# The gate of a feed-forward layer, merged in another order from the third chunk on

## The chip, the cores and the metric

The kernel runs on one core of a Trainium2 chip. Its engines work side by side, each through its own instructions in order: PE (TensorE, matmuls; PEld is its weight loads), DVE (VectorE), ACT (ScalarE), POOL (GpSimd) and SP, which issues the DMAs. PSUM is the memory that PE writes its products to; here it has eight banks of 128 x 512 floats. The metric is the time of one execution on the device in microseconds (us). Before the change it is 1264.36 us, the median of three runs (1263.34 to 1266.16).

## The reference

Attention over 8 batches of 8 heads, each with 512 local tokens and 32 global ones: a global token attends to all tokens, a local one to the global ones and to local ones at most 32 positions away. Its result `x` (4608 tokens of width 512) goes through a gated feed-forward layer of width 1536, which is what the change is in:

```python
gate = 1.0 / (1.0 + np.exp(-(x @ w_gate)))
val = x @ w_val
return (gate * val @ w_out).astype(np.float32)
```

## The kernel before

The tokens are worked in chunks. The first batch is two chunks of 256 tokens, each further batch one of 512, and the 256 global tokens are a last chunk. The feed-forward of a chunk is twelve items, one for each 128 columns of the hidden layer; the items of the first two chunks are interleaved, so items 0 to 23 are theirs, and from item 24 on each chunk's twelve follow one another. Matrices are split into a high and a low part in a reduced float format, and each product is three matmuls (high by high, low by high, high by low).

One item is: twelve matmuls into a PSUM tile `bank_g` (the gate's sum z), twelve into `bank_v` (the value), both at L380; then the gate and the product with the value; then a split of the result into `hh`; and, one item later, twelve matmuls of `hh` with `w_out` into four banks that collect the output (`bank_o`, L414). The stream yields after every four matmuls, and there the attention of a later chunk is slipped in: scores (L237, L317, L319), the row's maximum (L251, L322 to L324), exponentials (L254, L326, L327), scaling (L225), transposition on PE (L268, L335), the split of the transposed weights (L279 on ACT, then L280 on DVE), and the product with the values (L298, L299, L348), which leaves through L301 and L302. During the last two chunks there is no attention left to do.

The sigmoid is computed as half of (1 + |tanh(z/2)|) times exp(min(z, 0)); the half is taken with the output. For items from 24 on: ACT takes the tanh (L388) into `th`, DVE the minimum (L393) into `mn`, ACT the exponential of `mn` (L394) and the size of `th` (L395). L396 on DVE then makes (1 + `th`) x `mn`, and when `bank_v` is complete, L398 multiplies by it. L400 (ACT) and L401 (POOL) split the result.

`th` and `mn` have one buffer each, `hh` two. The PSUM tiles `bank_x`, `bank_y`, `bank_g` and `bank_v` share four banks: a new tile gets a bank when the last reader of the old one is done, and PE waits for that reader. The order of each engine's instructions is set when the program is built, by a scheduler that places each instruction by its dependences and an estimate of times, so a changed dependence can also move other instructions. SP, which issues the DMAs, and PE keep their order here; DVE, ACT and POOL do not.

Of the kernel before, what the change touches and what calls it, by code (L numbers as in the profile page):

```python
# [12 lines left out]
ALU = mybir.AluOpType  # L13
# [38 lines left out]
NF = DF // P  # L52
# [4 lines left out]
def kernel(ctx, tc, qk, v, w_gate, w_val, w_out, out_l, out_g):  # L57
    nc = tc.nc
# [306 lines left out]
    def ffn_stream(items):  # L365


        prev = None
        wo = None
        for n_it in range(len(items) + 1):  # L370
            if n_it < len(items):
                C, f = items[n_it]
                ntok, x0, xt = C["ntok"], C["x0"], C["xt"]()
                fs = slice(f * P, (f + 1) * P)
                for w, nm in ((wg, "bank_g"), (wv, "bank_v")):
                    acc = ps.tile([P, 512], F32, name=nm, tag="att", bufs=4)[:, 0:ntok]
                    n = 0
                    for a, c in ((0, 0), (1, 0), (0, 1)):
                        for t in range(KT):
                            nc.tensor.matmul(acc, w[a][:, t, fs], xt[:, c, t, x0:x0 + ntok],  # L380
                                             start=n == 0, stop=n == 11)
                            n += 1
                        if n < 12:
                            yield ntok / 512
                    if nm == "bank_g":
                        th = ffn.tile([P, 512], F32, name="th", bufs=1)[:, 0:ntok]
                        mn = ffn.tile([P, 512], F32, name="mn", bufs=1)[:, 0:ntok]
                        nc.scalar.activation(th, acc, AF.Tanh, scale=0.5)  # L388
                        if n_it < 2 * NF and n_it % 2:
                            nc.scalar.activation(mn, acc, AF.Relu, scale=-1.0)  # L390
                            nc.scalar.activation(mn, mn, AF.Exp, scale=-1.0)
                        else:
                            nc.vector.tensor_scalar(mn, acc, 0.0, None, op0=ALU.min)  # L393
                            nc.scalar.activation(mn, mn, AF.Exp)  # L394
                        nc.scalar.activation(th, th, AF.Abs)  # L395
                        nc.vector.scalar_tensor_tensor(th, th, 1.0, mn, op0=ALU.add, op1=ALU.mult)  # L396
                    else:
                        nc.vector.tensor_tensor(th, acc, th, op=ALU.mult)  # L398
                        hh = ffn.tile([P, 2, 512], F32R, name="hh", bufs=2)
                        nc.scalar.copy(hh[:, 0, 0:ntok], th)  # L400
                        nc.gpsimd.tensor_tensor(hh[:, 1, 0:ntok], th, hh[:, 0, 0:ntok].bitcast(F32), op=ALU.subtract)  # L401
                    yield ntok / 512
                if not (wo is not None and items[n_it - 1][1] == f):
                    wo = ffn.tile([P, 2, DM], F32R, name="wo", bufs=2)
                    nc.sync.dma_start(wo.bitcast(F32), wo_dram[f])
            if prev is not None:
                C2, f2, ph, pwo = prev
                nt = C2["ntok"] // P
                if f2 == 0:
                    C2["o"] = [ps.tile([P, DM], F32, name=f"bank_o{C2['o0'] + t}") for t in range(nt)]  # L410
                o_ps = C2["o"]
                for i, (a, c) in enumerate(((0, 0), (1, 0), (0, 1))):
                    for t in range(nt):
                        nc.tensor.matmul(o_ps[t], ph[:, a, t * P:(t + 1) * P], pwo[:, c],  # L414
                                         start=f2 == 0 and i == 0, stop=f2 == NF - 1 and i == 2)
                    if f2 == NF - 1 and i == 2:
                        for t in range(nt):
                            ob = ffn.tile([P, DM], F32, name="ob", bufs=2)
                            if t % 2:
                                nc.scalar.mul(ob, o_ps[t], 0.5)  # L420
                            else:
                                nc.vector.tensor_scalar(ob, o_ps[t], 0.5, None, op0=ALU.mult)
                            nc.sync.dma_start(C2["dst"][t * P:(t + 1) * P, :], ob)
                    yield nt / 4
            prev = (C, f, hh, wo) if n_it < len(items) else None
# [97 lines left out]
    for dt in ffn_stream(items):  # L523
        now += dt
        while queue and queue[0][0] <= now:
            queue.pop(0)[2]()
# [55 lines left out]
```

## Time and profile before

| | us |
|---|---|
| median of three runs | 1264.36 |
| the profiled execution, time | 1262.67 |
| its span, first to last instruction | 1260.8 |
| PE busy | 1223.5 (97%) |
| PE weight loads busy | 998.6 (79%) |
| DVE busy | 878.9 (70%) |
| ACT busy | 782.9 (62%) |
| POOL busy | 571.1 (45%) |

The mean granted clock of PE was 0.989; after the first 200 us it is 1.00. In the profile's rows, `out<-in` names the tiles, x is the count, and what stands behind an arrow is what ended the idle time before the instruction. Matmuls are pipelined, so the time of a group of them reaches a little past the start of the next. L numbers are lines of the kernel before the change.

### The profile page before, as it was taken

What the parts mean: (1) busy time and instruction counts of PE and PEld (TensorE: products, weight loads), DVE (VectorE), ACT (ScalarE), POOL (GpSimd) and SP (SyncE); (2) the same over time, 40 slices, a digit from 0 to 9 for tenths busy, and PEclk for the clock granted to TensorE, in tenths of its full rate; (3) what the DMA queues carried; (4) which work ended last, traced back from release to release, by engine and by line L of the source; (5) the groups of instructions that cost most, each with busy time, mean ns of one, the idle gap of its engine ahead of it and who ended that gap; (6) DMA issues with size and microseconds to landing.
All of it is one profiled execution on the core that took longest, in us unless ns stands there. A gap on an engine that the chain in (4) does not pass through costs nothing.

```text
span 1260.8 us, 20601 instructions
## 1 busy us (share of the span) xinstructions
PE 1223.5 (97%) x6884; PEld 998.6 (79%) x6884; DVE 878.9 (70%) x2433; ACT 782.9 (62%) x1899; POOL 571.1 (45%) x573
## 2 busy tenths in 40 slices
PE   8899989999999999999999999999999999999998
PEld 6677768788778877888788877888788877888897
DVE  6888977757876778758776778767875787632232
ACT  5686766756666666656765766656665666532333
POOL 2444545535555455545554455535554545311111
PEclk9798999999999999999999999999999999999999
DMA  6686754333333333333334333333333332122243
GB/s 232 215 264 219 255 172 125 107 97 108 92 103 113 113 92 108 109 106 112 100 86 120 121 100 100 108 112 109 91 107 114 108 92 88 51 84 67 67 134 117
DMA packets 59497, 151.90 MB, mean 120 GB/s; under 512 B 6144, under 2 KB 19456, under 8 KB 59392
## 3 DMA queue, kind: packets, MB, share of 16 engines
q1 hardware_dynamic: 59392, 150.59, 39.3%
q8 instruction: 54, 0.88, 0.3%
q14 instruction: 51, 0.42, 0.1%
HBM read 135.36 MB, written 15.20 MB: 119 GB/s over the span
## 4 chain that ended last, share of the span: by engine, by line
PE 73%; DVE 16%; ACT 6%; issue 4%; DMA 1%; POOL 0%; POOLq 0%; DVEq 0%; ACTq 0%; SPq 0%
PE bank_g L380 19%; PE bank_v L380 18%; PE bank_o L414 18%; PE bank_x L237 4%; PE bank_y L268 4%; DVE p_buf L225 3%; DVE th L396 2%; PE bank_y L335 2%; PE bank_x L348 2%; DVE pg_buf L225 2%; PE bank_x L298 2%; ACT s_sb L254 1%; PE bank_x L299 1%; PE bank_x L317 1%; DVE pt L280 1%
## 5 line engine op out<-in xcount | busy, mean ns | idle before, releaser
L380 PE MATMUL bank_g<-xt,wg 128*128 128x512 f32 (+1 forms) x1440 | 340.2, 371 | 1.8 <-DVE th L398 1.8
L380 PE MATMUL bank_v<-xt,wv 128*128 128x512 f32 (+1 forms) x1440 | 332.7, 368 | 3.0 <-DVE pt L280 2.7
L414 PE MATMUL bank_o<-wo,hh 128*128 128x512 f32 x1224 | 334.1, 404 | 0.8 <-ACT hh L400 0.4
L380 PEld LDWEIGHTS bank_g<-xt,wg 128*128 128x128 f32 x1440 | 238.6, 191 | 41.7 <-issue 3.5
L380 PEld LDWEIGHTS bank_v<-xt,wv 128*128 128x128 f32 x1440 | 237.8, 190 | 40.7 <-PE bank_y L319 3.1
L414 PEld LDWEIGHTS bank_o<-wo,hh 128*128 128x128 f32 x1224 | 214.1, 189 | 38.9 <-ACT hh L400 1.2
L401 POOL TENSOR_TENSOR hh<-th,hh 128x512 fp32r<-128x512 f32 (+1 forms) x120 | 137.6, 1147 | 200.7 <-ACT hh L400 199.8
L254 ACT ACTIVATE s_sb<-s_sb,nm 128x224 f32<-128x224 f32 x240 | 113.8, 475 | 142.9 <-DVE nm L251 141.8
L225 DVE TENSOR_SCALAR p_buf<-s_sb,r 128x128 f32<-128x128 f32 (+1 forms) x443 | 151.8, 386 | 4.2 <-PE bank_y L268 0.4
L393 DVE TENSOR_SCALAR mn<-bank_g 128x512 f32<-128x512 f32 (+1 forms) x108 | 67.3, 623 | 110.8 <-ACT th L388 109.4
L396 DVE SCALAR_TENSOR_TENSOR th<-th,mn 128x512 f32<-128x512 f32 (+1 forms) x120 | 102.0, 850 | 59.9 <-ACT mn L394 53.6
L206 POOL TENSOR_TENSOR kl<-qk_raw,qk_hi 128x704 fp32r<-128x704 f32 x52 | 88.4, 1700 | 116.0 <-ACT qk_hi L205 116.0
L303 POOL TENSOR_TENSOR x<-t 64x256 f32<-64x256 f32 x104 | 76.1, 732 | 142.7 <-DVE t L302 138.5
L388 ACT ACTIVATE th<-bank_g 128x512 f32<-128x512 f32 (+1 forms) x120 | 63.5, 530 | 98.0 <-PE bank_g L380 96.5
L400 ACT CAST hh<-th 128x512 fp32r<-128x512 f32 (+1 forms) x120 | 66.5, 554 | 68.6 <-DVE th L398 68.1
L251 DVE CUSTOM_DVE_ANT_0 s_sb<-bank_x,masks 128x224 f32<-128x224 f32 x240 | 83.8, 381 | 12.6 <-PE bank_x L237 8.2
L208 POOL TENSOR_TENSOR qk_hi<-qk_raw,qk_hi 64x256 fp32r<-64x256 f32 x104 | 87.8, 863 | 4.1
L268 PE MATMUL bank_y<-ident,p_buf 128*128 128x128 f32 x496 | 78.7, 279 | 9.4 <-DVE p_buf L225 5.1
L268 PEld LDWEIGHTS bank_y<-ident,p_buf 128*128 128x128 f32 x496 | 60.3, 142 | 29.5 <-ACT pg_buf L326 6.6
L257 DVE TENSOR_SCALAR r<-sm 128x2 f32<-128x2 f32 x128 | 29.3, 229 | 75.8 <-ACT s_sb L254 74.1
L205 ACT CAST qk_hi<-qk_raw 128x1248 fp32r<-128x1248 f32 x52 | 64.1, 1233 | 22.3 <-PE bank_y L319 22.2
L398 DVE TENSOR_TENSOR th<-bank_v,th 128x512 f32<-128x512 f32 (+1 forms) x120 | 72.4, 603 | 5.0 <-PE bank_v L380 1.3
(111 smaller groups left out, 1994.6 us busy)
## 6 DMA issues: line engine op xcount, KB each, us to landing
wo<-wo_dram SPq DMA_DIRECT2D x116, 512.0 KB, 3.5
qk_raw<-in_qk_dram SPq DMA_DIRECT2D x104, 312.0 KB, 4.5
v_raw<-in_v_dram SPq DMA_DIRECT2D x52, 256.0 KB, 2.6
out_dram<-ob SPq DMA_DIRECT2D x34, 256.0 KB, 2.9
xt<-in_w_gate_dram SPq DMA_DIRECT2D x12, 512.0 KB, 4.7
xt<-in_w_val_dram SPq DMA_DIRECT2D x12, 512.0 KB, 4.1
xt<-in_w_out_dram SPq DMA_DIRECT2D x12, 512.0 KB, 4.9
v_nat<-in_v_dram SPq DMA_DIRECT2D x8, 512.0 KB, 4.5
```

The costliest lines, as they stand in the source:

```text
L206: nc.gpsimd.tensor_tensor(kl, t[:, K0:Q1], hi[:, K0:Q1].bitcast(F32), op=ALU.subtract)
L208: nc.gpsimd.tensor_tensor(hi[64:128, r], t[64:128, r], hi[64:128, r].bitcast(F32), op=ALU.subtract)
L225: nc.vector.tensor_scalar(out, in_, by, None, op0=ALU.mult)
L251: anchor[0] = nc.vector.tensor_tensor_reduce(out=s_sb[:, i], in0=s_ps[:, i, 0:WIN], in1=masks[:, m], scale=-0.125, scalar=3.0e38, op0=ALU. ...
L254: nc.scalar.activation(s_sb[:, i], s_sb[:, i], AF.Exp, bias=nm[:, i:i + 1], scale=-1.0, accum_out=sm[:, i:i + 1])
L268: nc.tensor.transpose(pt_ps[:, 2 * i + t], pb[:, i, t * P:(t + 1) * P], ident)
L303: nc.gpsimd.tensor_tensor(dst, t0[:, :, 0], t0[:, :, 1], op=ALU.add)
L380: nc.tensor.matmul(acc, w[a][:, t, fs], xt[:, c, t, x0:x0 + ntok], start=n == 0, stop=n == 11)
L396: nc.vector.scalar_tensor_tensor(th, th, 1.0, mn, op0=ALU.add, op1=ALU.mult)
L398: nc.vector.tensor_tensor(th, acc, th, op=ALU.mult)
L401: nc.gpsimd.tensor_tensor(hh[:, 1, 0:ntok], th, hh[:, 0, 0:ntok].bitcast(F32), op=ALU.subtract)
L414: nc.tensor.matmul(o_ps[t], ph[:, a, t * P:(t + 1) * P], pwo[:, c], start=f2 == 0 and i == 0, stop=f2 == NF - 1 and i == 2)
```

## The change

For items from 24 on, the value's product is first multiplied by the exponential, in place in PSUM, and only then by one plus the tangent's size. The first two chunks keep the old order.

```diff
                         nc.scalar.activation(th, th, AF.Abs)
-                        nc.vector.scalar_tensor_tensor(th, th, 1.0, mn, op0=ALU.add, op1=ALU.mult)
+                        if n_it < 2 * NF:
+                            nc.vector.scalar_tensor_tensor(th, th, 1.0, mn, op0=ALU.add, op1=ALU.mult)
                     else:
-                        nc.vector.tensor_tensor(th, acc, th, op=ALU.mult)
+                        if n_it < 2 * NF:
+                            nc.vector.tensor_tensor(th, acc, th, op=ALU.mult)
+                        else:
+
+                            nc.vector.tensor_tensor(acc, acc, mn, op=ALU.mult)
+                            nc.vector.scalar_tensor_tensor(th, th, 1.0, acc, op0=ALU.add, op1=ALU.mult)
                         hh = ffn.tile([P, 2, 512], F32R, name="hh", bufs=2)
```

The two new lines are L403 and L404 of the changed kernel. Both read `bank_v`, so its bank comes free only after the second. The first place shown is on DVE, about the middle of the run, where a head's scaled weights (`p_buf`, L225) are done and the split of the transposed ones (`pt`, L280) follows; `mg` belongs to the softmax of the global tokens. Before:

```order
L225 TENSOR_SCALAR p_buf<-s_sb,r 128x96
L396 SCALAR_TENSOR_TENSOR th<-th,mn 128x512
L280 TENSOR_TENSOR pt<-bank_y,pt 128x512
L398 TENSOR_TENSOR th<-bank_v,th 128x512
L322 TENSOR_REDUCE mg<-bank_x 32x1
L323 TENSOR_REDUCE mg<-bank_y 32x1
L324 TENSOR_SCALAR mg<-mg 32x1
L329 TENSOR_SCALAR mg<-sg 32x1
```

The same place on DVE after the change:

```order
L225 TENSOR_SCALAR p_buf<-s_sb,r 128x96
L280 TENSOR_TENSOR pt<-bank_y,pt 128x512
L403 TENSOR_TENSOR bank_v<-bank_v,mn 128x512
L322 TENSOR_REDUCE mg<-bank_x 32x1
L404 SCALAR_TENSOR_TENSOR th<-th,bank_v 128x512
L323 TENSOR_REDUCE mg<-bank_y 32x1
L324 TENSOR_SCALAR mg<-mg 32x1
L302 TENSOR_TENSOR t_7206<-bank_x,t_7206 64x512
L329 TENSOR_SCALAR mg<-sg 32x1
```

The product of `th` and `mn` no longer stands ahead of L280; the last product now stands behind a reduction, L322, and L302 has moved up. The second place is on DVE too, a little earlier in the run, where the softmax weights of the global tokens (`pg_buf`, L225) are scaled. Before:

```order
L396 SCALAR_TENSOR_TENSOR th<-th,mn 128x512
L329 TENSOR_SCALAR mg<-sg 32x1
L398 TENSOR_TENSOR th<-bank_v,th 128x512
L302 TENSOR_TENSOR t_7014<-bank_x,t_7014 64x512
L280 TENSOR_TENSOR pt<-bank_y,pt 128x512
L330 RECIPROCAL mg<-mg 32x1
L225 TENSOR_SCALAR pg_buf<-pg_buf,mg 32x576
L251 ISA s_sb,nm<-bank_x,masks 128x224
```

And after:

```order
L329 TENSOR_SCALAR mg<-sg 32x1
L403 TENSOR_TENSOR bank_v<-bank_v,mn 128x512
L302 TENSOR_TENSOR t_7013<-bank_x,t_7013 64x512
L280 TENSOR_TENSOR pt<-bank_y,pt 128x512
L404 SCALAR_TENSOR_TENSOR th<-th,bank_v 128x512
L330 RECIPROCAL mg<-mg 32x1
L251 ISA s_sb,nm<-bank_x,masks 128x224
L251 ISA nm 128x1
L225 TENSOR_SCALAR pg_buf<-pg_buf,mg 32x576
```

Here the product of `th` and `mn` no longer stands ahead of L302 and L280; the last product and one L251 (a row's maximum, two rows) now stand between L280 and `pg_buf`. On ACT, at the first place, the copy that L302 needs (L301) now stands ahead of the split of `hh`. On POOL, at the same place, the second half of that split (L401 before, L407 after) now stands behind the two L208.

## The prediction

> **What bounds the kernel now.** I read the page's head and its chain of work first, then the busy time in two stretches, then who waits for whom inside them.
>
> ```profile
> PE 73%; DVE 16%; ACT 6%; issue 4%; DMA 1%; POOL 0%; POOLq 0%; DVEq 0%; ACTq 0%; SPq 0%
> ```
>
> TensorE (PE) carries 73% of the chain that ends last, VectorE (DVE) 16%. The profiled execution took 1262.67 us, of which its span is 1260.8 and 1.9 lies around it (the table above). The median of the runs shown, 1264.36, lies 1.69 higher, so I work out a difference on the trace and take it off the median.
>
> The change touches the items from the third chunk on. The first of their gates is on DVE at 271 us; up to 1110 us the attention of a later chunk runs beside them, after that the feed-forward is alone. Busy time by stretch (length, then PE, PEld, DVE, ACT, POOL):
>
> ```profile
> 270.00:1110.00 840.00, 830.95 (x4530) 676.49 (x4529) 628.57 (x1767) 552.51 (x1287) 425.54 (x429) 1.00 0.35 101
> 1110.00:1255.00 145.00, 144.81 (x762) 122.88 (x760) 40.13 (x72) 48.47 (x95) 22.91 (x23) 1.00 0.31 98
> ```
>
> PE idles 9.05 us in the first stretch and 0.19 in the second. The work itself is untouched, so at best the change returns PE's waits. Who PE waited for between 270 and 1110 us (total, times, longest):
>
> ```profile
> PE bank_x L298 <- DVE pt L280: 4.4, 11, 0.6
> PE bank_v L380 <- DVE pt L280: 2.7, 6, 0.5
> PE bank_y L335 <- DVE pg_buf L225: 1.2, 6, 0.2
> ```
>
> All three are DVE, and DVE works in order: what matters is what stands ahead of L280 and L225. The two instructions that the change replaces, in the same stretch (min/median/max ns; then by form with busy us, mean, idle before):
>
> ```profile
> L396 DVE SCALAR_TENSOR_TENSOR th<-th,mn x73: 691/693/1705, 271.1 to 1106.1; 128x512 f32<-128x512 f32 x73
> L398 DVE TENSOR_TENSOR th<-bank_v,th x73: 672/680/694, 272.3 to 1106.9; 128x512 f32<-128x512 f32 x73
> L396 DVE SCALAR_TENSOR_TENSOR th<-th,mn 128x512 f32<-128x512 f32 x73 | 73.1, 1001 | 37.9 <-ACT mn L394 37.9
> ```
>
> L396, both inputs in SBUF, takes 0.69 us at its shortest but 1.00 on average, and holds DVE's queue 37.9 us more while it waits for the exponential. L398, one operand in PSUM, is never over 0.694.
>
> **The change part by part.** It adds and removes no instruction: 96 pairs on DVE, of which 73 stand in this stretch, become 96 other pairs (L403 and L404 in the changed kernel's lines). No DMA is issued or moved, and the rows of PE and SP stay in their order.
>
> *What goes.* L396 leaves its early place in the queue and with it, in this stretch, 73.1 us of work and 37.9 of waiting ahead of L251, L280 and L302.
>
> *What comes.* The first new product (L403) writes PSUM, which no row shows DVE doing. Below it is bounded by the shortest L398, 0.67, above by two passes of it, 1.37; I take 0.68, L398's median, since size and inputs are the same. The second (L404) lies between L396's 0.69 and 1.70; I take 0.69, because the long runs are L396's alone and L398, which like L404 reads one operand from PSUM, has none. DVE's busy time in the stretch then falls by 73 x (1001 - 690) ns = 23 us, which is worth nothing by itself. What counts is PE's lost time at each place. The pattern repeats six times, once per chunk; I read the chunk around 600 us.
>
> Place A, around 608 us (start, duration):
>
> ```profile
> 606.15 0.59 ACT L279 CAST pt<-bank_y 128x512 fp32r<-128x512 f32 x1
> 606.22 1.29 DVE L396 SCALAR_TENSOR_TENSOR th<-th,mn 128x512 f32<-128x512 f32 x1 [0.23 <-ACT mn L394]
> 607.43 0.68 DVE L280 TENSOR_TENSOR pt<-bank_y,pt 128x512 fp32r<-128x512 f32 x1
> 608.03 0.68 DVE L398 TENSOR_TENSOR th<-bank_v,th 128x512 f32<-128x512 f32 x1
> 608.63 0.67 DVE L322 TENSOR_REDUCE mg<-bank_x 32x1 f32<-32x512 f32 x1
> 606.56 1.19 PE L414 MATMUL bank_o<-wo,hh 128*128 128x512 f32 x4
> 608.26 0.36 PE L298 MATMUL bank_x<-pt,vhl 128*128 128x256 f32 x1 [0.51 <-DVE pt L280]
> 608.81 1.10 PE L414 MATMUL bank_o<-wo,hh 128*128 128x512 f32 x4
> 609.75 0.60 PE L268 MATMUL bank_y<-ident,p_buf 128*128 128x128 f32 x4
> 611.08 1.72 POOL L208 TENSOR_TENSOR qk_hi<-qk_raw,qk_hi 64x256 fp32r<-64x256 f32 x2
> ```
>
> Four L414 matmuls hold PE 0.94 us to the next start (608.81 to 609.75), so L298 could have started at 607.50 and lost 0.76 (the 0.51 shown as idle leaves out the pipeline's tail). Without L396 ahead, L280 starts when ACT's L279 ends, 606.74, and ends at 607.42; PE follows a release by 0.15 (608.11 to 608.26), at 607.57. That returns 0.69. What is late next is L268: its tile takes the PSUM bank that the value's product leaves. Today L398 ends 1.04 before it. Afterwards L403, L322 and L404 follow L280 at the spacing of these rows, 0.60 each: L403 from 607.34, L322 from 607.94, L404 from 608.54 to 609.23. PE wants L268 0.69 earlier than today, at 609.06, and gets it at 609.38 with the same 0.15. Net at place A: 0.69 - 0.32 = **0.37**.
>
> Place B, around 596 us:
>
> ```profile
> 592.34 1.33 PE L380 MATMUL bank_v<-xt,wv 128*128 128x512 f32 x5
> 592.89 1.69 DVE L396 SCALAR_TENSOR_TENSOR th<-th,mn 128x512 f32<-128x512 f32 x1 [0.99 <-ACT mn L394]
> 594.34 0.59 ACT L279 CAST pt<-bank_y 128x512 fp32r<-128x512 f32 x1
> 595.89 0.67 DVE L280 TENSOR_TENSOR pt<-bank_y,pt 128x512 fp32r<-128x512 f32 x1
> 596.66 1.67 DVE L225 TENSOR_SCALAR pg_buf<-pg_buf,mg 32x576 f32<-32x576 f32 x1
> 595.35 1.11 PE L414 MATMUL bank_o<-wo,hh 128*128 128x512 f32 x4
> 596.62 0.38 PE L298 MATMUL bank_x<-pt,vhl 128*128 128x256 f32 x1 [0.16 <-DVE pt L280]
> 597.19 1.08 PE L414 MATMUL bank_o<-wo,hh 128*128 128x512 f32 x4
> 598.48 0.47 PE L335 MATMUL bank_y<-ident,pg_buf 32*128 32x32 f32 x5 [0.20 <-DVE pg_buf L225]
> ```
>
> By the same 0.94, L298 lost 0.33 (596.29 to 596.62) and L335 0.35 (598.13 to 598.48). Without L396, L403 starts at the last value matmul's end, 593.67; L302 and L280 follow, L280 from about 594.95, behind L279's end at 594.93, to 595.63: the **0.33** goes. Then L404, L330 and one L251 now stand ahead of L225, which so starts near 596.7, as today. If it takes its 1.67 again, PE gains nothing at L335 and loses the 0.33 again; if it is short, both go. I take half of the 0.35, **0.17**.
>
> Places C and D, around 625 and 639 us:
>
> ```profile
> 618.23 1.19 DVE L396 SCALAR_TENSOR_TENSOR th<-th,mn 128x512 f32<-128x512 f32 x1 [0.25 <-ACT mn L394]
> 619.34 0.38 DVE L251 CUSTOM_DVE_ANT_0 s_sb<-bank_x,masks 128x224 f32<-128x224 f32 x1
> 624.58 1.10 PE L380 MATMUL bank_g<-xt,wg 128*128 128x512 f32 x4
> 625.73 0.66 PE L268 MATMUL bank_y<-ident,p_buf 128*128 128x128 f32 x4
> 629.96 0.69 DVE L396 SCALAR_TENSOR_TENSOR th<-th,mn 128x512 f32<-128x512 f32 x1 [0.77 <-ACT mn L394]
> 637.01 1.96 DVE L225 TENSOR_SCALAR p_buf<-s_sb,r 128x128 f32<-128x128 f32 x4
> 637.37 1.29 POOL L218 TENSOR_TENSOR vhl<-v_raw,vhl 128x512 fp32r<-128x512 f32 x1
> 639.09 0.18 PE L319 MATMUL bank_y<-kl,qk_hi 128*32 128x32 f32 x1
> 639.71 1.64 PE L380 MATMUL bank_v<-xt,wv 128*128 128x512 f32 x6 [0.45 <-DVE pt L280]
> ```
>
> C loses 0.21 (625.52 to 625.73), behind a softmax chain that begins with the L251 of 619.34, itself right behind an L396; without the 1.19 and the 0.25 it starts over a microsecond earlier, so the **0.21** goes. D loses 0.59 (639.12 to 639.71): the chain to L280 starts at the L251 behind the L396 of 629.96, and goes 0.69 and 0.77 of waiting earlier. But the four L225 before L280 took 1.96 beside POOL's L218, and may again; I take half, **0.30**.
>
> Sum per chunk 0.37 + 0.33 + 0.17 + 0.21 + 0.30 = 1.38; six chunks, 8.3 us. In two more places per chunk of the built program L268 takes the bank of the value's product; one has little room, and I set 0.1 for it: 0.6 in six.
>
> *Where nothing is gained or lost.* The last item, where nothing covers the gate's chain:
>
> ```profile
> 1251.10 1.59 PE L380 MATMUL bank_v<-xt,wv 128*128 128x256 f32 x12
> 1252.75 0.42 DVE L396 SCALAR_TENSOR_TENSOR th<-th,mn 128x256 f32<-128x256 f32 x1 [0.55 <-ACT mn L394]
> 1253.28 0.42 DVE L398 TENSOR_TENSOR th<-bank_v,th 128x256 f32<-128x256 f32 x1
> ```
>
> The value is complete at 1252.69, before L396 starts: the new pair can stand where the old one stands, and costs nothing. Earlier items of the second stretch end up to 0.7 later on DVE, hidden by an item's matmuls, in which PE idles only 0.19. On POOL the hidden layer's split moves behind two L208 at place A; its reader on PE comes an item later, so I cost it at nothing; without that cover it is their time, 1.72 (611.08).
>
> [...]
>
> **The rivals.** *All waits go.* L225 short at B and D, L404 in time at A: (0.76 + 0.33 + 0.35 + 0.21 + 0.59) x 6 = 13.4, so 1251.0. For it: DVE's queue gets back 23 us of work and 38 of waits. Against: L404 must come 0.32 earlier at A than I find.
>
> *Given back at the next wait.* Only 0.33 at B and 0.21 at C stay, 3.2, and the three bank waits per chunk take 1.2: 2.0 net, 1262.4. For it: L404 lands before the very instructions that feed L335 and L268.
>
> *The bank comes too late.* Between L403's end and L404's end stand 0.60 + 0.69 = 1.29, plus 0.15 to PE: 1.44 against today's 1.04. If L403 starts no earlier than L398 does, PE waits 0.40 at three L268 per chunk, 7.2 in all, less the 3.2 of B and C: 4.0 slower, 1268.4. It decides where L403 starts less than 0.40 earlier than L398; at A I find 0.68. An L403 of 1.37 has the same effect. [...]
>
> **How the numbers follow.** 8.3 - 0.6 = 7.7 off: 1264.36 - 7.7 = 1256.7 (1255.0 by the profiled execution). Chances: forecast 0.52, all waits gone 0.13, given back 0.20, bank too late 0.15. About 0.2%, 2.5 us, is what a measurement of this kernel can tell from no change. Faster 0.66, same 0.19, slower 0.15. The range goes from just under the first rival, 1250.0, to 1266.5, half way into the last.
>
> **What would show it.** Right: L404's longest run near 0.69; the waits on L280 in the stretch well under 7.1 us; L268 newly waiting for L404, some 0.3 at A. Wrong: L403 over 0.9, L268 waiting 0.4 at three places per chunk, or L225 still 1.67 before L335.

## The result, and the profile after

The changed kernel takes 1250.80 us, the median of four runs (1249.65 to 1254.35); beside it the kernel before took 1264.89 (four runs). The ratio is 0.9903, with a 95% interval of 0.9890 to 0.9916: 1.0% faster, 14.1 us by the medians. The forecast was 7.7 us faster, 1256.7, with a range of 1250.0 to 1266.5. The sign and the range held, the size did not: the rival *all waits go*, at 1251.0, comes closest. The profiled execution took 1249.65 us, with a span of 1247.8 against 1260.8. One execution of a later run, e5_one_more_pass, took 4080 us; it is left out of that run's ratio.

The busy time by stretch of the changed kernel (length, then PE, PEld, DVE, ACT, POOL), and the head of its chain of waits:

```profile
270.00:1097.00 827.00, 826.28 (x4523) 676.49 (x4523) 600.50 (x1766) 549.75 (x1286) 420.69 (x429) 1.00 0.36 103
1097.00:1242.00 145.00, 144.83 (x763) 123.30 (x762) 40.30 (x72) 48.58 (x96) 23.30 (x24) 1.00 0.30 98
PE 79%; DVE 11%; issue 6%; ACT 2%; POOL 1%; DMA 0%; POOLq 0%; DVEq 0%; ACTq 0%
```

In the stretch with attention PE idles 0.72 us where it idled 9.05, and the view of who PE waits for, from 270 to 1100 us, has no row left: the three rows on L280 and `pg_buf` are gone. The last stretch idles 0.17 (0.19 before). Of the 13.0 us between the spans, 11.7 lie in the six chunks with attention, 0.8 ahead of them and 0.5 behind them. DVE has 28 us less to do in 13 us less of time (628.57 before).

What is left are short waits of PE's weight loads, and the two new products cost what was taken for them (the waits; then by form: count, busy us, mean ns, idle before):

```profile
PEld bank_y L268 <- ACT pg_buf L326: 8.2, 23, 0.5
PEld bank_x L298 <- DVE pt L280: 2.5, 12, 0.3
PEld bank_y L268 <- DVE th L404: 1.9, 6, 0.5
```

```profile
L403 DVE TENSOR_TENSOR bank_v<-bank_v,mn 128x512 f32<-128x512 f32 x73 | 50.3, 689 | 14.2 <-PE bank_v L380 9.0 <-ACT s_sb L254 5.1
L404 DVE SCALAR_TENSOR_TENSOR th<-th,bank_v 128x512 f32<-128x512 f32 x73 | 49.2, 674 | 0.7
L225 DVE TENSOR_SCALAR pg_buf<-pg_buf,mg 32x576 f32<-32x576 f32 x48 | 34.1, 711 | 1.3
```

L403 was priced at 0.68 and takes 0.689 on average, L404 at 0.69 and takes 0.674. `pg_buf`, one of the two open costs, became shorter (0.910 before).

Place A in the timeline of the changed kernel (start, duration; the same instructions as in the prediction):

```profile
600.90 0.59 ACT L279 CAST pt<-bank_y 128x512 fp32r<-128x512 f32 x1
601.52 0.69 DVE L280 TENSOR_TENSOR pt<-bank_y,pt 128x512 fp32r<-128x512 f32 x1 [0.78 <-ACT pt L279]
603.32 0.67 DVE L404 SCALAR_TENSOR_TENSOR th<-th,bank_v 128x512 f32<-128x512 f32 x1
602.12 1.19 PE L420 MATMUL bank_o<-wo,hh 128*128 128x512 f32 x4
603.15 0.28 PE L298 MATMUL bank_x<-pt,vhl 128*128 128x256 f32 x1
604.55 0.60 PE L268 MATMUL bank_y<-ident,p_buf 128*128 128x128 f32 x4
```

The mark to read by is the group of four `bank_o` matmuls ahead of L298. Before, ACT's L279 ended 0.18 after that group's start (606.74 against 606.56); now it ends 0.63 before it (601.49 against 602.12). So everything behind L279 is 0.81 earlier than the prediction held it, L404 ends at 603.99, and L268 at 604.55 has no wait. The group takes 1.03 to L298's start here and not 0.94, so the loss at A had been 1.70 - 1.03 = 0.67, not 0.76.

Place B and place D of the changed kernel:

```profile
591.30 0.67 DVE L280 TENSOR_TENSOR pt<-bank_y,pt 128x512 fp32r<-128x512 f32 x1
592.87 0.50 DVE L225 TENSOR_SCALAR pg_buf<-pg_buf,mg 32x576 f32<-32x576 f32 x1
592.53 0.28 PE L298 MATMUL bank_x<-pt,vhl 128*128 128x256 f32 x1
594.02 0.49 PE L335 MATMUL bank_y<-ident,pg_buf 32*128 32x32 f32 x5
...
630.93 1.84 DVE L225 TENSOR_SCALAR p_buf<-s_sb,r 128x128 f32<-128x128 f32 x4 [0.49 <-PE bank_y L268]
632.70 0.67 DVE L280 TENSOR_TENSOR pt<-bank_y,pt 128x512 fp32r<-128x512 f32 x1
633.42 0.18 PE L319 MATMUL bank_y<-kl,qk_hi 128*32 128x32 f32 x1
633.52 1.87 PE L380 MATMUL bank_v<-xt,wv 128*128 128x512 f32 x7
```

At B neither L298 nor L335 waits, and `pg_buf` takes 0.50 instead of 1.67. At D the four L225 are as long as before (1.84 against 1.96), but they and L280 are early enough: L380 follows L319 by 0.10, where it followed by 0.62.

### The profile page after: what moved, and what is told of

Read it like the earlier page. It is cut to its first block, busy times and chain, and to the rows that moved or that the text cites. A ratio compares the mean times of both kernels' runs of the same rounds, so it can differ in the third digit from the quotient of the medians.

```text
span 1247.8 us, 20555 instructions
## 1 busy us (share of the span) xinstructions
PE 1219.8 (98%) x6884; PEld 999.5 (80%) x6884; DVE 851.3 (68%) x2433; ACT 781.0 (63%) x1899; POOL 567.2 (45%) x573
## 4 chain that ended last, share of the span: by engine, by line
PE 79%; DVE 11%; issue 6%; ACT 2%; POOL 1%; DMA 0%; POOLq 0%; DVEq 0%; ACTq 0%
PE bank_v L380 21%; PE bank_g L380 20%; PE bank_o L420 19%; PE bank_x L237 5%; PE bank_y L268 4%; DVE p_buf L225 3%; PE bank_x L348 2%; PE bank_y L335 2%; PE bank_x L317 2%; PE bank_x L299 2%; PE bank_x L298 2%; DVE xt L148 1%; DVE xt L147 1%; DVE xt L140 1%; DVE mg L322 1%
## 5 line engine op out<-in xcount | busy, mean ns | idle before, releaser
L380 PE MATMUL bank_g<-xt,wg 128*128 128x512 f32 (+1 forms) x1440 | 340.3, 371 | 1.8 <-DVE th L400 1.8
L380 PE MATMUL bank_v<-xt,wv 128*128 128x512 f32 (+1 forms) x1440 | 332.7, 369 | 0.3 <-DVE mn L393 0.3
L380 PEld LDWEIGHTS bank_g<-xt,wg 128*128 128x128 f32 x1440 | 238.6, 191 | 41.5 <-issue 3.4
L380 PEld LDWEIGHTS bank_v<-xt,wv 128*128 128x128 f32 x1440 | 237.9, 190 | 37.7 <-issue 1.1
L407 POOL TENSOR_TENSOR hh<-th,hh 128x512 fp32r<-128x512 f32 (+1 forms) x120 | 138.1, 1151 | 219.3 <-ACT hh L406 217.1
L254 ACT ACTIVATE s_sb<-s_sb,nm 128x224 f32<-128x224 f32 x240 | 113.8, 475 | 95.1 <-DVE nm L251 94.5
L225 DVE TENSOR_SCALAR p_buf<-s_sb,r 128x128 f32<-128x128 f32 (+1 forms) x443 | 158.2, 402 | 7.1 <-PE bank_y L268 3.1
L206 POOL TENSOR_TENSOR kl<-qk_raw,qk_hi 128x704 fp32r<-128x704 f32 x52 | 88.3, 1698 | 137.6 <-ACT qk_hi L205 137.6
L303 POOL TENSOR_TENSOR x<-t 64x256 f32<-64x256 f32 x104 | 76.5, 736 | 104.1 <-DVE t L302 101.1
L388 ACT ACTIVATE th<-bank_g 128x512 f32<-128x512 f32 (+1 forms) x120 | 63.4, 529 | 91.5 <-PE bank_g L380 88.2
L251 DVE CUSTOM_DVE_ANT_0 s_sb<-bank_x,masks 128x224 f32<-128x224 f32 x240 | 84.5, 381 | 18.6 <-PE bank_x L237 14.5
L218 POOL TENSOR_TENSOR vhl<-v_raw,vhl 128x512 fp32r<-128x512 f32 x52 | 67.7, 1302 | 58.6 <-ACT vhl L217 57.6
L268 PE MATMUL bank_y<-ident,p_buf 128*128 128x128 f32 x496 | 79.4, 281 | 9.6 <-DVE p_buf L225 4.9
L403 DVE TENSOR_TENSOR bank_v<-bank_v,mn 128x512 f32<-128x512 f32 (+1 forms) x96 | 63.2, 658 | 36.3 <-PE bank_v L380 30.7
L268 PEld LDWEIGHTS bank_y<-ident,p_buf 128*128 128x128 f32 x496 | 59.1, 142 | 32.6 <-ACT pg_buf L326 10.3
L208 POOL TENSOR_TENSOR qk_hi<-qk_raw,qk_hi 64x256 fp32r<-64x256 f32 x104 | 82.1, 809 | 4.1
```

The lines of the kernel that those rows point to most:

```text
L206: nc.gpsimd.tensor_tensor(kl, t[:, K0:Q1], hi[:, K0:Q1].bitcast(F32), op=ALU.subtract)
L208: nc.gpsimd.tensor_tensor(hi[64:128, r], t[64:128, r], hi[64:128, r].bitcast(F32), op=ALU.subtract)
L218: nc.gpsimd.tensor_tensor(vhl[:, :, D:2 * D], t, vhl[:, :, 0:D].bitcast(F32), op=ALU.subtract)
L225: nc.vector.tensor_scalar(out, in_, by, None, op0=ALU.mult)
L251: anchor[0] = nc.vector.tensor_tensor_reduce(out=s_sb[:, i], in0=s_ps[:, i, 0:WIN], in1=masks[:, m], scale=-0.125, scalar=3.0e38, op0=ALU. ...
L254: nc.scalar.activation(s_sb[:, i], s_sb[:, i], AF.Exp, bias=nm[:, i:i + 1], scale=-1.0, accum_out=sm[:, i:i + 1])
```

## The experiments

Two questions were open. Are the places A to D separate, as the sum took them, or does a lead at one place reach the next? And is the cost of L396 its place in DVE's queue, or the long runs of an instruction with both inputs in SBUF? The runs below stand beside runs of the kernel before; "idle" is 400 us less the busy time of PE in the stretch from 400 to 800 us (three chunks), from the view by stretches; "six chunks" is the time from the first matmul of item 24 to that of item 96 in the trace. Items are counted 0 to 11 in a chunk; A's gate is item 5, B's item 4, C's and D's chains begin at items 6 and 7. In the traces of the runs that leave the first two chunks as they are, item 24 begins between 264.40 and 268.27 us, so up to 4 us between two executions arise ahead of the change; the length of the six chunks is free of that.

| run | what differs | median us | before beside it | ratio (95%) | idle us | six chunks us |
|---|---|---|---|---|---|---|
| kernel before | | | | | 4.12 | 834.88 |
| changed kernel | | 1250.80 | 1264.89 | 0.9903 (0.9890 to 0.9916) | 0.38 | 823.16 |
| g3_changed_again | nothing | 1252.48 | 1263.11 | 0.9909 (0.9895 to 0.9922) | 0.26 | 823.03 |
| f2_item4 | new order at item 4 alone | 1253.29 | 1263.62 | 0.9919 (0.9901 to 0.9937) | 1.50 | 826.66 |
| f1_item5 | new order at item 5 alone | 1266.13 | 1263.62 | 1.0020 (1.0011 to 1.0030) | 4.34 | 839.00 |
| f3_items45 | items 4 and 5 | 1253.41 | 1263.62 | 0.9917 (0.9902 to 0.9933) | 0.24 | 825.67 |
| f4_not4567 | all but items 4 to 7 | 1270.09 | 1263.62 | 1.0049 (1.0033 to 1.0064) | 4.36 | 840.33 |
| e1_product_in_sbuf | new place, both inputs in SBUF | 1261.11 | 1263.43 | 0.9977 (0.9965 to 0.9989) | 2.81 | 832.70 |
| e3_early_from_psum | old place, one input in PSUM | 1254.71 | 1263.43 | 0.9924 (0.9909 to 0.9940) | 0.36 | 825.66 |
| g1_item4_late_sbuf | as e1, at item 4 alone | 1254.55 | 1263.11 | 0.9925 (0.9912 to 0.9939) | 0.45 | 825.80 |
| g2_item4_early_psum | as e3, at item 4 alone | 1256.70 | 1263.11 | 0.9944 (0.9931 to 0.9956) | 1.48 | 829.78 |
| e5_one_more_pass | bank held one product longer | 1273.42 | 1263.43 | 1.0076 (1.0064 to 1.0088) | 5.88 | 845.53 |
| e4_all_items | new order in the first two chunks too | 1246.61 | 1263.43 | 0.9863 (0.9848 to 0.9878) | 0.33 | 823.14 |

### Which places: f2_item4, f1_item5, f3_items45, f4_not4567

These four are the changed kernel with another condition; on DVE the gates of all other items stand as in the kernel before, but near a changed item rows of the attention have moved too (`pg_buf` and L342 in f2, L302 in f1). For item 4:

```diff
-                        if n_it < 2 * NF:
+                        if n_it < 2 * NF or n_it >= 8 * NF or n_it % NF != 4:
```

(in both places; `!= 5` for item 5, `not in (4, 5)` for both, `in (4, 5, 6, 7)` for all but those). The old order's first product is L397 there.

> Items are counted 0 to 11 in each chunk. The new order stands only at item 4 of the six chunks with attention beside them, the item whose gate is at place B; all other items keep the old one, so at place A (item 5) L396 stands ahead of L280 as before. If the places are independent, as the prediction took them, only B's 0.33 (with the pg_buf wait 0.68) comes back: 2.0 to 4.1 us, 1260.8 to 1262.9. If lead is carried (my theory now: at B VectorE gets to the next softmax almost 2 us earlier, so ScalarE gets earlier to tanh, exponential and split at A), A's loss of 0.76 goes too although nothing is changed there: 1.44 x 6 = 8.6, about 1256.3, and PE's waits for L280 in 270 to 1100 us shrink from 11 to 2 or fewer.

Item 4 alone brings 10.3 us, more than was given for independent places and even than for a carried lead; in the trace its six chunks are 8.2 us shorter than before, where a carried lead was given 8.6. Place A of this run, where nothing was changed:

```profile
601.42 0.59 ACT L279 CAST pt<-bank_y 128x512 fp32r<-128x512 f32 x1
601.50 1.29 DVE L397 SCALAR_TENSOR_TENSOR th<-th,mn 128x512 f32<-128x512 f32 x1 [0.23 <-ACT mn L394]
602.71 0.68 DVE L280 TENSOR_TENSOR pt<-bank_y,pt 128x512 fp32r<-128x512 f32 x1
602.65 1.19 PE L420 MATMUL bank_o<-wo,hh 128*128 128x512 f32 x4
603.67 0.28 PE L298 MATMUL bank_x<-pt,vhl 128*128 128x256 f32 x1
```

The early product is as long as before (1.29) and waits as long for the exponential (0.23), and yet L298 has no wait. L280 starts 0.06 after the `bank_o` group, where it started 0.87 after it. The lead comes from B: DVE reaches the softmax behind B earlier, ACT its exponentials (L254), and behind them in ACT's queue stand the tanh, the exponential and the split (L388, L394, L279) of A. On PE, ACT and POOL the order of this run is that of the kernel before, so moves on those engines have no part in its gain. Of the waits in the three chunks the view shows only D's:

```profile
PE bank_v L380 <- DVE pt L280: 1.4, 3, 0.5
```

> The new order stands only at item 5 of the six chunks with attention beside them, place A; ScalarE comes to A as late as before the change. By the prediction's own step (L268 waits about 0.3 for the product's bank) 0.37 x 6 = 2.2 come back: 1262.7, and the trace shows L268 waiting for L404 about 0.2 to 0.3, six times. If that step was wrong by its price and not by its time of start, there is no such wait and 0.69 to 0.76 x 6 = 4.1 to 4.6 come back: 1260.5.

Item 5 alone is 0.2% slower, which neither theory gave. Place A of this run and the microseconds behind it:

```profile
607.50 0.59 ACT L279 CAST pt<-bank_y 128x512 fp32r<-128x512 f32 x1
609.92 0.67 DVE L404 SCALAR_TENSOR_TENSOR th<-th,bank_v 128x512 f32<-128x512 f32 x1
610.64 0.66 PE L268 MATMUL bank_y<-ident,p_buf 128*128 128x128 f32 x4
612.75 1.63 DVE L225 TENSOR_SCALAR pg_buf<-pg_buf,mg 32x576 f32<-32x576 f32 x1
612.77 1.30 POOL L407 TENSOR_TENSOR hh<-th,hh 128x512 fp32r<-128x512 f32 x1
614.31 0.67 DVE L280 TENSOR_TENSOR pt<-bank_y,pt 128x512 fp32r<-128x512 f32 x1
615.03 0.39 PE L298 MATMUL bank_x<-pt,vhl 128*128 128x256 f32 x1 [0.50 <-DVE pt L280]
```

With ACT as late as before (L279 ends 0.20 after the group at 607.89), A behaves as the prediction worked it out: L298 no longer waits, and L268 starts 1.14 after the four `bank_o` matmuls ahead of it (609.50 in the timeline), 0.2 later than the 0.94 of those rows. So the working at A was right under its assumption. What it had not seen follows: L302 now stands ahead of `pg_buf`, `pg_buf` comes later and meets L407 on POOL, which had moved behind the two L208; it takes 1.63 instead of 0.97, and the next L298, which had no loss before, waits. A's gain is paid back there: a chunk in the middle is 0.3 longer than before. The last two of the six are 1.7 and 1.2 longer; there DVE also stands behind the output's store (7.7 us in this run, 4.4 in the kernel before).

> The new order at items 4 and 5 of the six chunks, places B and A together. Independent places as priced: (0.33 + 0.17 + 0.37) x 6 = 5.2, 1259.7, with L268 waiting some 0.3 for L404 at A. Lead carried: (0.68 + 0.76) x 6 = 8.6 or a little more, at most 1256.3, and no wait of L268 for L404. If it is no faster than the run with item 4 alone, item 5's change is worth nothing once B is early.

Together they are as fast as item 4 alone within the intervals, but D's wait is gone as well: PE idles 0.24, as little as with all items changed. So the two items do all that the change does inside an undisturbed chunk. That its six chunks are still 2.5 us longer than the changed kernel's comes from two chunks outside the 400 us; in one of them DVE stands behind the output's store (`ob` has two buffers, and the copy at the head of the queue waits until a DMA has read one):

```profile
829.98 0.69 DVE L428 TENSOR_SCALAR ob<-bank_o 128x512 f32<-128x512 f32 x1 [2.96 <-DMA out_dram<-ob]
```

Such waits sum to 6.9 us on DVE in this run and 0.6 in the changed kernel (270 to 1100 us). They are longer wherever most items keep the old order (4.4 to 8.2 us, against 0.4 to 2.5 in the other runs); why the store is then late was not tried.

> The new order at items 0 to 3 and 8 to 11 of the six chunks, the old one at items 4 to 7, whose gates stand at A to D. Independent places: nothing comes back, 1264.9 within 0.2%. Lead carried: what these eight items gain on VectorE (some 0.3 us of work and 0.5 of waiting each) can reach B from the items ahead of it, at most B's 0.33 and part of A's 0.76: 1260 to 1264.

The other eight items alone make the kernel 0.5% slower, which neither theory gave. All waits at A, B and D stay, and short ones are added; weight loads that wait for the global tokens' exponential sum to

```profile
PEld bank_y L268 <- ACT pg_buf L326: 9.9, 23, 0.5
```

where the kernel before has 4.5 us, 12 times. The changed kernel has nearly as many (8.2), so the other items of the change cost a little there. In the trace the six chunks are 5.5 us longer than before. In the chunks in the middle it is some 0.7 each: two new waits of L268 for L326, 0.22 each, and a short one for L404 make most of it. The fifth chunk is 2.7 longer, and again an L319 waits there behind the store. The profiled execution, 1266.46, is the fastest of the six; what the others have beyond it stays open.

### Place or kind of operand: e1_product_in_sbuf, e3_early_from_psum, g1_item4_late_sbuf, g2_item4_early_psum

Late, but with both inputs in SBUF (against the changed kernel):

```diff
-                            nc.vector.tensor_tensor(acc, acc, mn, op=ALU.mult)
-                            nc.vector.scalar_tensor_tensor(th, th, 1.0, acc, op0=ALU.add, op1=ALU.mult)
+                            nc.vector.tensor_tensor(mn, acc, mn, op=ALU.mult)
+                            nc.vector.scalar_tensor_tensor(th, th, 1.0, mn, op0=ALU.add, op1=ALU.mult)
```

Early, but with one input in PSUM (against the kernel before, whose products it keeps; they are L402 and L404 there):

```diff
-                            nc.scalar.activation(mn, mn, AF.Exp)
+                            late = n_it >= 2 * NF
+                            if late:
+                                mn2 = acc
+                            else:
+                                mn2 = mn
+                            nc.scalar.activation(mn2, mn, AF.Exp)
+                            mn = mn2
```

> The new order as changed, but the value's product with the exponential is written to mn in SBUF, and L404 reads th and mn, both in SBUF; the bank is free after L403. The places in VectorE's queue are the same as in the changed kernel. If the gain is the place in the queue, this is as fast as the changed kernel, 1250.8 within 2.5 us, although L404 shows runs of up to 1.7 us again. If the gain is the end of the long runs of an instruction with two SBUF inputs, they come back here and with them much of the loss: 1255 to 1265. L268 has no wait for the product any more, which is worth the 6 x 0.5 that the changed kernel's trace shows at most as 1.9 us.

> The old order, early in the queue, but from the third chunk on the exponential is written into the gate's own PSUM tile, so the early product reads one operand from PSUM and one from SBUF. It still waits for the exponential ahead of L251, L280 and L302; it should have no long runs (0.69, against 1.00 on average). Long runs as cause: place A gets 0.60 and B 1.0 of VectorE's time back, so most of the gain is here, 1251 to 1255. Place in the queue as cause: the waits for the exponential (38 us in the stretch) stay and most of the loss with them, 1259 to 1264.9. The gate's bank is held about 1.5 us longer, which may add waits of PE for a bank.

The kind of operand weighs more than the place. With the new place and two SBUF inputs most of the gain is gone (0.2% faster, within the range given for the long runs). With the old place and one PSUM input most of it is there (0.8%), although the first product still waits 35.9 us in front of the others, 34.4 of it for the exponential:

```profile
L402 DVE SCALAR_TENSOR_TENSOR th<-th,bank_g 128x512 f32<-128x512 f32 x73 | 50.2, 687 | 35.9 <-ACT bank_g L399 34.4
```

Its mean is 0.687 where L396 took 1.00. But e3 does not change the operand alone: in its build PE takes four matmuls of L298 and L299 later, behind the whole value product and two of `bank_o`, at item 4 and at one more place of each chunk, and on DVE `pg_buf` stands ahead of L302 and L280 at B. In its undisturbed chunks e3 is as fast as the changed kernel. The 2.5 us by which its six chunks are longer are nearly all two waits of PE, 1.97 and 0.47, at an L319 that takes the gate's bank, which L402 now holds while it stands behind the output's store:

```profile
831.76 0.69 DVE L428 TENSOR_SCALAR ob<-bank_o 128x512 f32<-128x512 f32 x1 [2.76 <-DMA out_dram<-ob]
834.59 0.20 PE L319 MATMUL bank_y<-qk_hi 128*32 128x32 f32 x1 [1.97 <-DVE th L402]
```

e1 is the cleaner run: PE, ACT and POOL keep the changed kernel's order, and on DVE only rows of L225 have moved. In e1 the collision comes back, but mostly on POOL's side: L206 takes 1.942 on average there, where it takes 1.698 in the changed kernel, and L404 0.705, where it takes 0.674. POOL's L206 and DVE's L404 of e1 (start, duration), and all runs of L206 and of L404 there between 270 and 1100 us (min/median/max ns):

```profile
562.89 2.60 POOL L206 TENSOR_TENSOR kl<-qk_raw,qk_hi 128x704 fp32r<-128x704 f32 x1 [7.93 <-ACT qk_hi L205]
563.26 0.67 DVE L404 SCALAR_TENSOR_TENSOR th<-th,mn 128x512 f32<-128x512 f32 x1
L206 POOL TENSOR_TENSOR kl<-qk_raw,qk_hi x46: 1688/1703/2605, 283.9 to 1060.3; 128x704 fp32r<-128x704 f32 x46
L404 DVE SCALAR_TENSOR_TENSOR th<-th,mn x72: 666/672/1779, 275.0 to 1098.1; 128x512 f32<-128x512 f32 x72
```

L206 takes 1.71 at this place in the changed kernel. What stands behind it on POOL, L407 and the next L303, is late in turn, and through ACT's copy, DVE's L302 and the softmax behind it the delay comes to PE, at an L298 that waits in neither of the two kernels:

```profile
569.38 0.59 ACT L301 COPY t<-bank_x 64x512 f32<-64x512 f32 x1 [0.77 <-POOL x L303]
578.79 0.39 PE L298 MATMUL bank_x<-pt,vhl 128*128 128x256 f32 x1 [0.54 <-DVE pt L280]
```

So e1 does not fail at A or B; it collides elsewhere.

> The new place at item 4 of the six chunks alone, with the product written to mn in SBUF, so that both inputs of L404 are in SBUF there; everywhere else the old order. If at place B the early place in the queue was the cost, this is as fast as the run with item 4 alone and the product in PSUM, 1253.3 within 2.5, and PE idles about 1.5 us between 400 and 800 us (before 4.12). If it was the kind of operand, L404 or the POOL instruction beside it runs long here and PE idles 3 us or more: 1258 to 1264.

> The old order everywhere, but at item 4 of the six chunks the exponential is written into the gate's PSUM tile, so that the early product has one operand in SBUF there and cannot run 1.69 us. If either remedy is enough at place B, PE idles about 1.5 us between 400 and 800 us and the time is 1253.3 within 2.5. If the wait at the head of VectorE's queue (0.99 at B) is what costs, B's 0.33 and A's 0.76 stay: 1260 to 1264.

These are the same two edits, limited to item 4 of the six chunks. At B either remedy is enough: both bring most of the gain (g2 ends 0.9 us above the range given for it), and PE idles 0.45 and 1.48. In g2 the wait for the exponential is still there, and L298 behind it has none:

```profile
590.52 0.69 DVE L402 SCALAR_TENSOR_TENSOR th<-th,bank_g 128x512 f32<-128x512 f32 x1 [0.96 <-ACT bank_g L399]
```

L402 starts as far ahead of the `bank_o` group before L298 as L396 did (2.57 and 2.46), waits as long, and is 1.00 shorter; so by these rows what hurt at B was the 1.00 that L396 took beyond its 0.69, not the 0.99 that it waited. It is not shown alone, since g2's build has the same moves at item 4 as e3's. That g2's six chunks are 3.1 us longer than f2's lies mostly in the last two, where DVE stands behind the store (8.2 us). In g1 POOL's L303 took 1.25 beside L404, instead of 0.73, and PE did not come to wait for it:

```profile
594.61 0.67 DVE L404 SCALAR_TENSOR_TENSOR th<-th,mn 128x512 f32<-128x512 f32 x1
594.63 1.25 POOL L303 TENSOR_TENSOR x<-t 64x256 f32<-64x256 f32 x1
```

### The bank: e5_one_more_pass

```diff
                             nc.vector.tensor_tensor(acc, acc, mn, op=ALU.mult)
+                            nc.vector.tensor_scalar(acc, acc, 1.0, None, op0=ALU.mult)
                             nc.vector.scalar_tensor_tensor(th, th, 1.0, acc, op0=ALU.add, op1=ALU.mult)
```

> The changed kernel with one more instruction between L403 and L404, a multiplication of the product by one in place in PSUM, so the bank comes free about 0.6 to 0.7 us later and VectorE gets 73 x 0.67 = 49 us more work in the stretch. The rival 'the bank comes too late' is priced by it: at A L268 started 0.56 after L404's end, of which 0.15 is the shortest delay, so there are 0.41 of room, and L268 should now wait about 0.2 there and more at the places that already waited (0.4 each): up to 0.9 x 6 = 5 us slower than the changed kernel, 1251 to 1256. If the extra pass delays the softmax as well, lead is lost and it goes further back, towards 1260.

It is 0.8% slower than the kernel before, and so 1.7% slower than the changed one: more than was expected at its worst. Who PE waited for (L405 is the last product here):

```profile
PE bank_y L268 <- DVE th L405: 8.7, 17, 0.6
PE bank_x L298 <- DVE pt L280: 4.8, 14, 0.6
```

The mechanism of the rival *the bank comes too late* is real, and at three places per chunk, as it said. The changed kernel stays out of it by little: at A, L404 ends 0.56 before L268 starts, and at one other place of each chunk L268's weight load does wait for it (the 1.9 us above).

### A faster version: e4_all_items

The changed kernel with `n_it < 0` for `n_it < 2 * NF` in its two conditions, so that the first two chunks have the new order too.

> The new order for the items of the first two chunks too, which are 256 tokens long, interleaved and worked beside attention. If waits behind the early product cost PE there as well, it is 0.5 to 3 us faster than the changed kernel, 1248 to 1250.3. If the first 270 us are bound by loads and by PE itself, it is the same, 1250.8 within 1.

That is more than was expected. With 1246.61 us it beats both kernels: 1.4% under the kernel before, and the intervals of the two ratios to it do not meet (0.9878 against 0.9890). The gain is in the first two chunks: item 24 begins at 259.65, where it began at 265.16, and the six chunks are as long as in the changed kernel. Two of PE's waits for DVE from 150 to 266 us in the changed kernel, and then the two in this one:

```profile
PE bank_x L298 <- DVE pt L280: 2.9, 4, 1.0
PE bank_g L380 <- DVE th L400: 1.8, 1, 1.8
```

```profile
PE bank_y L268 <- DVE p_buf L225: 1.5, 1, 1.5
PE bank_x L298 <- DVE pt L280: 0.3, 1, 0.3
```

### The common measure: g3_changed_again

> The changed kernel once more, as the common measure for the runs of this study: 1250.8 within 2.5, PE idle below 0.5 us between 400 and 800 us.

It agrees with the first measurement (0.9909 against 0.9903). The two medians of the same kernel are 1.7 us apart (1252.48 and 1250.80), so differences of that size between medians of this study are not to be read.

## Why the prediction was right, and where its size failed

**What bounds the kernel: right.** PE, and the stretch up to 1110 us, and the three waits on L280 and `pg_buf`. The change returned them, and the tail, costed at nothing, gave next to nothing (0.19 idle before, 0.17 now; 0.5 of its length).

**The prices of the new products: right.** 0.68 and 0.69 taken, 0.689 and 0.674 measured; the upper bounds of 1.37 and 1.70 were never near. L404, with one input in PSUM, takes 0.674 where L396's shortest run with none took 0.691, so the choice of the row was right.

**Place A: this step failed.** "L280 starts when ACT's L279 ends, 606.74" held ACT at its old times while DVE's queue ahead of it was emptied at B. Relative to PE the split came 0.81 earlier. With that the 0.32 of waiting for the bank was never due, and A gave its whole 0.67 instead of 0.37. f1 shows that 0.2 of that wait comes where ACT is really late; f2 shows that A's loss goes by B alone. The sign *L268 newly waiting for L404, some 0.3 at A* did not come at A.

**The halves at B and D: the same step.** Half of 0.35 was taken for L335 and half of 0.59 for D, for fear of a long L225. At B `pg_buf` was short, because the second half of the split (L407 on POOL) now comes 0.49 after it started; 1.29 shrank to 1.02, a gain of 0.27. At D L225 was long, as feared, and it did not matter: it started 0.41 earlier against L319 and was 0.12 shorter, L280 came 0.53 earlier, and 0.52 came back. B's L298 gave 0.33 as forecast.

**C and the allowance of 0.1.** C's 0.21 went, but short waits of L268 for L326 came at two other places of a chunk; the weight loads' wait for it rose from 4.5 to 8.2 us. Each new wait puts L268 1.15 after the four matmuls ahead of it, where 0.93 is free of a wait. The allowance for L404's bank was about right: the six L268 that wait for it start 0.92 to 1.20 after theirs, 0.46 in all where 0.6 was set. What had no term is the waits for L326.

**The sum, then.** The six chunks run from the first matmul of item 24 to that of item 96; for the kernel before and the changed one these end at

```profile
1100.80 3.04 PE L380 MATMUL bank_g<-xt,wg 128*128 128x512 f32 x12
```

```profile
1088.32 3.04 PE L380 MATMUL bank_g<-xt,wg 128*128 128x512 f32 x12
```

and begin at 265.92 and 265.16, so they are 834.88 and 823.16 long: 11.7 less, 1.95 per chunk, where the forecast had 1.38 - 0.10 = 1.28. A, B's two and D returned 0.67 + 0.33 + 0.27 + 0.52 = 1.79 where 1.17 was set for them; these are the terms that were set too small. C with the new waits of some 0.22 at two other places, and 0.08 for L404's bank, makes about -0.31 where 0.21 - 0.10 was set. These single waits sum to 1.48; the other 0.47 per chunk is spread over gaps that I did not assign. The 2.4 us between 11.7 and the 14.1 of the medians lie outside these chunks (0.8 ahead of item 24 and 0.5 behind item 96) and in the spread of the runs.

**The mechanism that was named: half right.** The prediction took L396's place in the queue as the cause, and its long runs as part of it; it called the 23 us of DVE's time "worth nothing by itself". e3 takes away the long runs and leaves the early place, though not every other place, and brings 8.7 us. The wait for the exponential, 37.9 us of the rows, is nearly free in the chunks in the middle: in e3 PE idles 0.36 in three of them, with 34.4 of that wait still there in the whole stretch. What the change needed above all is that its last product reads PSUM (e1 against the changed kernel, 0.9977 against 0.9903). The later place adds nothing in the undisturbed chunks, where PE idles as little in both; the 2.5 us of e3's longer chunks are the two waits behind the output's store. By the ratios the two kernels are 2 to 3 us apart, and their intervals overlap.

**The rivals.** *All waits go* had 0.13 and the condition "L404 0.32 earlier at A"; it was met, through ACT. That its 13.4 comes so near 14.1 is partly luck: four of its places returned 1.79 per chunk where it set 2.03, new waits took C's 0.21 back, and 2.4 of the 14.1 lie outside the six chunks. *Given back at the next wait* is what f1 does by itself. *The bank comes too late* is what e5 does.

## What to carry to other kernels

Places at which an engine waits for another should not be summed as if each had its own clock: take the first of them, shift everything behind it on all engines by what it returns, and only then price the next. Here a product on VectorE with both inputs in SBUF took 1.00 on average where its shortest run is 0.691 (L396), or the GpSimd instruction beside it took longer (L206 in e1, up to 2.605 where its median is 1.703); with one operand in PSUM the product took 0.674 at the new place (L404) and 0.687 at the old one (e3). Where a trace shows such long runs, one operand in PSUM is worth a try. A change that helps at one item can be neutral or harmful at others (items 4, 5 and the eight others here), so it is worth trying on parts.

## What the runs showed of the hardware

Where L396, with two SBUF inputs, meets an instruction of POOL, it is the one that runs long. Of its 73 runs in the kernel before (270 to 1110 us), the 43 with no POOL instruction beside them take 0.69; the other 30 start 0.50 to 0.65 after an L206, L218 or L363 of POOL and take 1.19 to 1.71, while POOL's instruction takes 1.70 to 1.71 (L206) or 1.29 to 1.30 (the two others). In e1 it was the other way round at the place shown: L404 kept its 0.67 and POOL's L206, which had begun 0.37 earlier, took 2.60 instead of 1.71; yet L404's longest run there is 1.779. With one input in PSUM none of L404's 73 runs in the changed kernel is above 0.690; 17 of them overlap an L206, take 0.67 and leave it its 1.70 to 1.71:

```profile
L404 DVE SCALAR_TENSOR_TENSOR th<-th,bank_v x73: 665/668/690, 272.3 to 1095.1; 128x512 f32<-128x512 f32 x73
```

Which of the two runs long does not follow from whose row begins first: POOL's begins first in those 30 meetings and at e1's place, while `pg_buf` is the one that runs long at B before (1.67) and in f1 (1.63) though its row begins 0.07 and 0.02 ahead of POOL's. Spans on POOL are rough in such a profile, so what decides it was not shown.

Long runs are not L396's alone. L225 reads one tile from SBUF and a factor for each row, and its four 128 x 128 pieces take 0.91 at 599.83 in the changed kernel and 2.62 at 568.00, there beside POOL's L218 and L407.

DVE also wrote PSUM in place, which no row of before showed: L403, which reads and writes `bank_v`, took 0.689 against 0.681 for a product that also has one input in PSUM and one in SBUF and is written to SBUF (L398 before).
